# A soft threshold written as a minimum plus a relu of ACT, and weight conversion moved out of the second batch's first stage

## The chip, the cores and the metric

The kernel runs on one core of a Trainium2 chip. The time is that of one execution on the device, in microseconds (us); less is better. A core has five engines with a queue each, worked off in order: PE (matmuls), DVE (vector work), ACT (activations, copies and the issue of some transfers), POOL, and SP, which here only issues transfers. An instruction that waits holds up all that stands behind it in its own queue. Matmuls write to PSUM banks; DVE and ACT carry the results on to SBUF.

## The reference, cut to what matters

```python
X = np.fft.rfft(x, axis=1)                       # x: (2, 3008, 256)
Yr = Xr @ w_r - Xi @ w_i + b_r
Yi = Xr @ w_i + Xi @ w_r + b_i
Y = sign(Y) * max(abs(Y) - 0.01, 0)              # of both parts: the soft threshold
x = np.fft.irfft(Y, n=3008, axis=1)
...
x = (h * clip(h + 3, 0, 6) / 6) @ w_out          # h = x @ w_in, 2048 wide
x = (silu(x @ w_gate) * (x @ w_val)) @ w_out2    # 1536 wide
```

The change lies in the first five lines and in the preparation of the weights `w_in` and `w_out`.

## The kernel before

The Fourier transform of each batch is done in factors. The *first stage* (`pre`, 8 pieces n = 0 to 7 for batch 0 and 8 to 15 for batch 1) multiplies a 96x1024 piece of x with a small table; the two halves of the result are copied from PSUM, half 0 by ACT (L245) and half 1 by DVE (L247), and sent to the scratch tensor Bd. The rest goes in 12 *rounds* p = 0 to 11, six for each batch (`ORDER`), of four frequencies each. The functions of a round:

- `s2` (S): matmuls with a table (L284) in two parts, dh = 0 and 1. For each part ACT makes the high half xh (L288) and its negative (L289), DVE the low half xl (L118), and ACT the negative of that (L291), which is put off to just before the next step by the list `later`.
- `ln` (L), in two halves h: first one step of the weight conversion if any is left, then 24 matmuls (L113 to L115), then on DVE the bias is added (yb, L319), clipped to plus and minus 0.01 (yc, L321) and subtracted (yp, L323).
- `ia` (A), in two halves: matmuls of yp with a table (L330), a copy by ACT (cs, L331), and after the second half the transfer to the scratch tensor Cd (L333).

The order is written out by hand in `seq`. Round p is: L(p) half 0, A(p-1) half 0, a first-stage piece, S(p+1) part 0, S(p+1) part 1, L(p) half 1, a first-stage piece, A(p-1) half 1. First-stage pieces 11 to 15 stand in rounds 0 to 2. From round 8 (`FROM`) on, *units* of the next layer are put between these steps: matmuls ph and acc (L113 to L115), relu r (L430, ACT), product r (L431, DVE), and the split into gh (L449, ACT) and gl (L118, DVE). Just before round 8 stands `post` of the first block (L416), which needs ct, read back from Cd (L404). Batch 1's rounds begin at round 6, so "round 8" is batch 1's third.

*Weight conversion* (`conv1`, 32 pieces) makes two fp32 halves of 64-bit floats. One step works on five pieces at once: DVE makes a piece's low half (L179), ACT another's high half (L175), ACT the mask of the next (L156), DVE the words of one (L164, L165, L166, L172), and SP loads one more (L151). A step runs inside each half of `ln`, inside `pre` for pieces n > 8, and in a unit whenever its weights are due (`conv1.at < 2 * n + 6`), until all is done.

Of the kernel before, what the change touches and what calls it, by code (L numbers as in the profile page):

```python
# [9 lines left out]
F32 = mybir.dt.float32  # L10
# [3 lines left out]
AF = mybir.ActivationFunctionType  # L14
ALU = mybir.AluOpType
# [11 lines left out]
LAM = 0.01  # L27
# [50 lines left out]
def fourier_moe_kernel(ctx: ExitStack, tc: tile.TileContext, x, lin, bias, w1, w2, fwd1, inv2, fwd2,  # L78
                       inv1, out):
    nc = tc.nc  # L80

    def pool(stack, name, side):
        return stack.enter_context(tc.tile_pool(name=name, bufs=1, side=side))
# [28 lines left out]
    def mm3(o, wh, wl, xh, xl, start, stop):  # L112
        nc.tensor.matmul(o, wl, xh, start=start, stop=False)  # L113
        nc.tensor.matmul(o, wh, xl, start=False, stop=False)  # L114
        nc.tensor.matmul(o, wh, xh, start=False, stop=stop)  # L115
# [72 lines left out]
    def pieces(p, name, src, nf, n, into):  # L188
        out = []
        for f in range(nf):  # L190
            t = [p.tile([128, n, 256], F32R, name=f"{name}{i}_{f}") for i in "hl"]
            into[f] = t
            out += [(src[:, f, j], t[0][:, j], t[1][:, j]) for j in range(n)]
        return Convert(out)
# [3 lines left out]
    ap_ = pool(attn_stack, "attn", "right")  # L198
    linh = ap_.tile([128, 2, 2, DIM], F32R, name="linh")
    linl = ap_.tile([128, 2, 2, DIM], F32R, name="linl")  # L200
    bias_sb = ap_.tile([128, DIM], F32, name="bias_sb")

    def ring4(name):
        return ap_.tile([128, 4 * DIM], F32, tag="bc", name=name, bufs=4)


    NT = NJ // 4
    xt = {}

    def load_x(n):  # L210
        b, i = divmod(n, NT)
        if b < NB:
            xt[n] = xs_p.tile([128, 4 * DIM], F32, tag="xah" if n % 2 else "xal", name=f"x{b}_{i}", bufs=2)
            nc.sync.dma_start(xt[n][:QP], x[b][:, i * 4 * DIM : (i + 1) * 4 * DIM])
# [5 lines left out]
    p = psf[0]([128, 512], "p0")  # L220
    for n in range(3):
        nc.tensor.matmul(p, zeros[:, :128], zeros, start=True, stop=True)
    conv1 = pieces(w1p, "w1", w1, KF1, 2, W1)

    def prepare():
        lin_st = ap_.tile([128, 2, 2, DIM], F32, tag="z", name="lin_st", bufs=3)
        nc.gpsimd.dma_start(lin_st, lin)
        nc.gpsimd.dma_start(bias_sb, bias)
        nc.gpsimd.dma_start(inv2_sb, inv2)
        for dh in range(2):  # L230
            for k in range(2):
                hi, lo, st = linh[:, dh, k], linl[:, dh, k], lin_st[:, dh, k]
                nc.gpsimd.tensor_copy(hi, st)
                nc.gpsimd.tensor_tensor(out=lo, in0=st, in1=hi.bitcast(F32), op=ALU.subtract)

    def pre(n):
        b, i = divmod(n, NT)
        load_x(n + 3)
        bs = ring4(f"bs{b}_{i}")
        for h in range(2):  # L240
            p = psf[0]([GW, 512], f"p1_{b}_{i}_{h}")
            nc.tensor.matmul(p, fwd1_sb, xt[n][:QP, h * 512 : (h + 1) * 512], start=True, stop=True)
            o = bs[:GW, h * 512 : (h + 1) * 512]
            if h == 0:
                nc.scalar.copy(o, p)  # L245
            else:
                nc.vector.tensor_copy(o, p)  # L247
        sent()
        out_b.append(lambda: nc.scalar.dma_start(Bd[b][:, i * 4 * DIM : (i + 1) * 4 * DIM], bs[:GW]))
        if i == NT - 1:  # L250
            sent()
# [3 lines left out]
    def sent():  # L255

        for g in out_b:
            g()
        out_b.clear()
# [3 lines left out]
    m_t, z_t, n_t, X, yp, cs = {}, {}, {}, {}, {}, {}  # L263

    def table(tag, src, Q, name, bufs):
        t = ap_.tile([128, 4, 128], F32, tag=tag, name=name, bufs=bufs)
        nc.sync.dma_start(t, src[:, Q * 512 : (Q + 1) * 512].rearrange("r (g c) -> r g c", g=4))
        return t

    def load_q(b, Q):  # L270
        if (b, Q) in z_t or Q >= NQ:
            return
        if Q not in m_t:
            m_t[Q] = table("m", fwd2, Q, f"m{Q}", 6)
        z_t[b, Q] = ap_.tile([128, 4, DIM], F32, tag="z", name=f"z{b}_{Q}", bufs=3)
        nc.sync.dma_start(z_t[b, Q], bview[b][:, Q * 4 : Q * 4 + 4, :])

    def s2(b, Q, dh):

        if dh == 0:  # L280
            X[b, Q] = [ap_.tile([128, 2, 4, 3 * K2], F32R, tag=f"x{k}", name=f"x{k}_{b}_{Q}", bufs=2) for k in "hl"]
        p = psf[0]([128, 4, 128], f"p2_{b}_{Q}_{dh}")
        for g in range(4):
            nc.tensor.matmul(p[:, g, :], z_t[b, Q][:, g, dh * 128 : (dh + 1) * 128], m_t[Q][:, g, :],  # L284
                             start=True, stop=True)
        hi, lo = (t[:, dh, :, K2:] for t in X[b, Q])
        nhi, nlo = (t[:, dh, :, :K2] for t in X[b, Q])
        nc.scalar.copy(hi, p)  # L288
        nc.scalar.mul(nhi, p[:, :, K2:], -1.0)  # L289
        low(lo, p, hi)  # L290
        later.append(lambda: nc.scalar.mul(nlo, X[b, Q][1][:, dh, :, 2 * K2 :].bitcast(F32), -1.0))  # L291

    later = []
# [8 lines left out]
    def ln(b, Q, h):  # L302

        if Q not in n_t:
            n_t[Q] = table("n", inv1, Q, f"n{Q}", 6)
        if not conv1.done():
            conv1.step()
        p = psf[0]([128, 2, DIM], f"p3_{b}_{Q}_{h}")
        xh, xl = X[b, Q]
        for i in range(2):  # L310
            g = 2 * h + i
            n = 0
            for dh in range(2):
                for k, at in ((0, K2), (1, 0)):
                    sl = (slice(None), dh, g, slice(at, at + 128))
                    mm3(p[:, i, :], xh[sl], xl[sl], linh[:, dh, k], linl[:, dh, k], n == 0, n == 3)
                    n += 1
        yb = xs_p.tile([128, 2, DIM], F32, tag="r", name=f"yb{b}_{Q}_{h}", bufs=3)
        nc.vector.tensor_tensor(out=yb, in0=p, in1=bias_sb.unsqueeze(1).to_broadcast([128, 2, DIM]), op=ALU.add)  # L319
        yc = xs_p.tile([128, 2, DIM], F32, tag="r", name=f"yc{b}_{Q}_{h}", bufs=3)  # L320
        nc.vector.tensor_scalar(yc, yb, -LAM, LAM, op0=ALU.max, op1=ALU.min)  # L321
        yp[b, Q, h] = ap_.tile([128, 2, DIM], F32, tag="yp", name=f"yp{b}_{Q}_{h}", bufs=3)
        nc.vector.tensor_tensor(out=yp[b, Q, h], in0=yb, in1=yc, op=ALU.subtract)  # L323

    def ia(b, Q, h):
        if h == 0:
# [14 lines left out]
    def ahead(p):  # L341
        if p < len(ORDER):
            load_q(*ORDER[p])

    def S(p):
        def first():
            ahead(p + 1)
            s2(*ORDER[p], 0)
        return [first, lambda: s2(*ORDER[p], 1)] if p < len(ORDER) else []

    def L(p):
        return [lambda h=h: ln(*ORDER[p], h) for h in range(2)]

    def A(p):
        return [lambda h=h: ia(*ORDER[p], h) for h in range(2)] if p >= 0 else [lambda: None] * 2

    def pre_conv(n):
        pre(n)
        if n > NT:
            conv1.step()  # L360

    P = [lambda n=n: pre_conv(n) for n in range(NB * NT)]
    seq = P[:1] + [prepare] + P[1:NT] + [lambda: load_q(0, 0)] + P[NT : NT + 3] + S(0)
    rest = P[NT + 3 :]
    for p in range(len(ORDER)):
        l, a = L(p), A(p - 1)
        some, rest = rest[:2], rest[2:]
        u = [lambda: unit()] if p >= FROM else []
        seq += [l[0], a[0]] + u + some[:1] + S(p + 1)[:1] + u + S(p + 1)[1:] + [l[1]] + u + some[1:] + [a[1]] + u
        if p == NQ:  # L370
            seq += [lambda: load_ct(blocks[0])]
        if p == FROM - 1:
            seq += [lambda: few.__setitem__(0, True)]
            seq += [lambda: post(blocks[0], 0), lambda: post(blocks[0], 1)]
# [101 lines left out]
    def unit():  # L476

        n = at[0]
        at[0] += 1

        for _ in range(2):
            if conv1.at < 2 * n + 6 and not conv1.done():
                conv1.step()
        if 0 <= n - 1 < len(units):
            lower(units[n - 1])
        if n < len(units):
            k, f = units[n]
            state[units[n]] = project1(k, f, ntok(k))
        if n >= 2:
            outp(units[n - 2])  # L490
        if n < len(units):
            for step in extra.get(units[n], ()):
                step()
        for f in more:
            f(n)
# [303 lines left out]
```

## Time and profile before

| | before |
|---|---|
| time, median of 3 runs (lowest to highest) | 1256.91 us (1256.39 to 1258.61) |
| time of the profiled execution | 1257.64 us |
| its span, first to last instruction | 1255.8 us |
| PE busy | 1233.0 us, 98% |
| DVE busy | 845.7 us, 67% |
| ACT busy | 679.5 us, 54% |
| POOL busy | 6.3 us |
| chain that ended last, by engine | PE 90%, DVE 5%, DMA 2%, ACT 2% |

The shares are averages over stages. The change touches the first 210 us or so, where DVE and ACT feed PE in short steps; the rest of the span is two layers of long matmuls. PE's busy time is modelled from pipelined matmuls, so a PE that reads 98% can still have lost time.

### The profile page before, as it was taken

How to read it: one execution, taken by the hardware profiler on the slowest of the kernel's cores; microseconds unless marked ns; L12 is line 12 of the kernel's file. 1: busy time of each engine (PE TensorE's matmuls, PEld its weight loads, DVE VectorE, ACT ScalarE, POOL GpSimd, SP SyncE). 2: the span in 40 equal slices, each digit the busy share in tenths (PEclk: the TensorE clock that was granted, in tenths of full speed). 3: DMA queues.
4: the chain of work that ended last, by engine and by line, in shares of the span. 5: the costliest groups of instructions: out<-in, count | busy, mean ns of one | idle time of the engine just before them, and what ended most of it. 6: DMA issues, size and time to landing. Idle time of an engine off the chain costs nothing.

```text
span 1255.8 us, 15966 instructions
## 1 busy us (share of the span) xinstructions
PE 1233.0 (98%) x5914; PEld 1035.6 (82%) x5914; DVE 845.7 (67%) x1492; ACT 679.5 (54%) x1216; POOL 6.3 (0%) x15
## 2 busy tenths in 40 slices
PE   8889999999999999999999999999999999999998
PEld 2789898788888888888889878888888888888997
DVE  2588767676666676676666567677676676666665
ACT  2344445455555555555555465566556665555554
POOL 1000000000000000000000000000000000000000
PEclk9899999999999999999999999999999999999999
DMA  9965511231321221232132054554544644544551
GB/s 300 277 220 160 169 42 64 93 99 63 97 95 55 90 89 49 93 99 83 54 104 91 25 212 151 201 187 169 203 166 156 229 171 153 214 153 164 207 184 72
DMA packets 50286, 172.85 MB, mean 138 GB/s; under 512 B 4752, under 2 KB 18160, under 8 KB 39456
## 3 DMA queue, kind: packets, MB, share of 16 engines
q1 hardware_dynamic: 41856, 158.55, 36.7%
q10 hardware_dynamic: 8128, 12.58, 2.9%
q8 instruction: 46, 0.75, 0.2%
q0 software_dynamic: 224, 0.69, 0.2%
q14 instruction: 32, 0.26, 0.1%
HBM read 132.75 MB, written 39.06 MB: 137 GB/s over the span
## 4 chain that ended last, share of the span: by engine, by line
PE 90%; DVE 5%; DMA 2%; ACT 2%; issue 1%; ACTq 0%; DVEq 0%; SPq 0%
PE acc L114 12%; PE acc L115 12%; PE acc L113 12%; PE ph L113 7%; PE ph L115 7%; PE ph L114 7%; PE P L652 5%; PE P L654 5%; PE P L653 5%; PE p L416 3%; PE Tb L652 3%; PE Tb L653 3%; PE Tb L654 3%; PE Q L652 1%; PE Q L654 1%; PE Q L653 1%
## 5 line engine op out<-in xcount | busy, mean ns | idle before, releaser
L118 DVE TENSOR_TENSOR gl<-r,gh 128x512 fp32r<-128x512 f32 (+1 forms) x192 | 130.1, 677 | 79.8 <-ACT gh L449 78.6
L430 ACT ACTIVATE r<-ph,three 128x512 f32<-128x512 f32 (+1 forms) x192 | 130.2, 678 | 96.5 <-PE ph L115 78.3
L431 DVE SCALAR_TENSOR_TENSOR r<-r,ph 128x512 f32<-128x512 f32 (+1 forms) x192 | 129.4, 674 | 61.1 <-ACT r L430 60.4
L449 ACT CAST gh<-r 128x512 fp32r<-128x512 f32 (+1 forms) x192 | 117.4, 611 | 87.5 <-DVE r L431 86.6
L113 PE MATMUL ph<-xah,w1l 128*128 128x512 f32 (+1 forms) x384 | 152.2, 396 | 0.7 <-DVE w1l L179 0.7
L113 PE MATMUL acc<-gh,w1l 128*128 128x512 f32 (+1 forms) x384 | 148.3, 386 | 1.0 <-ACT gh L449 1.0
L114 PE MATMUL acc<-gl,w1h 128*128 128x512 f32 (+1 forms) x384 | 148.3, 386 | 0.6 <-DVE gl L118 0.5
L115 PE MATMUL ph<-xah,w1h 128*128 128x512 f32 (+1 forms) x384 | 148.2, 386 | 0.0
L114 PE MATMUL ph<-xal,w1h 128*128 128x512 f32 (+1 forms) x384 | 148.2, 386 | 0.0
L115 PE MATMUL acc<-gh,w1h 128*128 128x512 f32 (+1 forms) x384 | 148.1, 386 | 0.0
L118 DVE TENSOR_TENSOR gl<-s,gh 128x512 fp32r<-128x512 f32 (+1 forms) x144 | 97.2, 675 | 49.5 <-ACT gh L676 49.5
L652 PE MATMUL P<-xo,slot 128*128 128x512 f32 (+1 forms) x288 | 111.3, 386 | 1.7 <-DVE g L722 0.8
L114 PE MATMUL acc<-gl,slot 128*128 128x512 f32 (+1 forms) x288 | 111.1, 386 | 0.3 <-DVE gl L118 0.2
L113 PE MATMUL acc<-gh,slot 128*128 128x512 f32 (+1 forms) x288 | 111.0, 385 | 0.0
L654 PE MATMUL P<-xo,slot 128*128 128x512 f32 (+1 forms) x288 | 110.9, 385 | 0.0
L653 PE MATMUL P<-xo,slot 128*128 128x512 f32 (+1 forms) x288 | 110.9, 385 | 0.0
L115 PE MATMUL acc<-gh,slot 128*128 128x512 f32 (+1 forms) x288 | 110.9, 385 | 0.0
L718 ACT ACTIVATE s<-g 128x512 f32<-128x512 f32 (+1 forms) x72 | 44.9, 623 | 93.2 <-DVE g L716 93.2
L676 ACT CAST gh<-s 128x512 fp32r<-128x512 f32 (+1 forms) x144 | 88.1, 612 | 1.8 <-DVE s L735 1.6
L114 PEld LDWEIGHTS acc<-gl,w1h 128*128 128x128 f32 x384 | 72.1, 188 | 15.3 <-DVE gl L118 1.7
L113 PEld LDWEIGHTS acc<-gh,w1l 128*128 128x128 f32 x384 | 72.1, 188 | 15.1 <-ACT gh L449 1.5
L113 PEld LDWEIGHTS ph<-xah,w1l 128*128 128x128 f32 x384 | 72.2, 188 | 14.2 <-issue 0.8
(95 smaller groups left out, 2292.9 us busy)
## 6 DMA issues: line engine op xcount, KB each, us to landing
slot<-Wd SPq DMA_DIRECT2D x72, 1152.0 KB, 5.0
st<-in_w SPq DMA_DIRECT2D x68, 256.0 KB, 3.2
Wd<-slot SPq DMA_DIRECT2D x12, 1152.0 KB, 4.7
x<-in_x SPq DMA_DIRECT2D x16, 384.0 KB, 6.2
Bd<-bs ACTq DMA_DIRECT2D x16, 384.0 KB, 5.1
z<-Bd SPq DMA_DIRECT2D x12, 512.0 KB, 5.5
Cd<-cs ACTq DMA_DIRECT2D x12, 512.0 KB, 3.3
Xd<-x SPq DMA_DIRECT2D x20, 256.0 KB, 2.1
```

The source lines that it names most:

```text
L113: nc.tensor.matmul(o, wl, xh, start=start, stop=False)
L114: nc.tensor.matmul(o, wh, xl, start=False, stop=False)
L115: nc.tensor.matmul(o, wh, xh, start=False, stop=stop)
L118: nc.vector.tensor_tensor(out=o, in0=full, in1=hi.bitcast(F32), op=ALU.subtract)
L430: nc.scalar.activation(r[:, :n], p[:, :n], AF.Relu, bias=three)
L431: nc.vector.scalar_tensor_tensor(out=r[:, :n], in0=r[:, :n], scalar=6.0, in1=p[:, :n], op0=ALU.min, op1=ALU.mult)
L449: nc.scalar.copy(hi[:, :n], g[:, :n])
L652: nc.tensor.matmul(o, wl, x[:, 0, :n], start=start, stop=False, skip_group_check=not start)
L653: nc.tensor.matmul(o, wh, x[:, 1, :n], start=False, stop=False, skip_group_check=not start)
L654: nc.tensor.matmul(o, wh, x[:, 0, :n], start=False, stop=True, skip_group_check=not start)
L676: nc.scalar.copy(hi[:, :nb], t[:, :nb])
L718: nc.scalar.activation(s0[:, :n], h, AF.Silu)
```

## The change

Four edits, all in the first two hundred microseconds.

1. The soft threshold is written min(y + 0.01, 0) + relu(y - 0.01). The 0.01 is added to the bias once, on POOL (in `prepare`); DVE adds the bias (yb), ACT makes the relu (yc) with the bias tile `edge2` = -0.02, and DVE joins them with one instruction (yp). That last one is put in the list `later`, which is worked off just before the next step.
2. For batch 1 both halves of a first-stage piece are copied by ACT.
3. `pre` runs no conversion step any more (7 steps, of pieces 9 to 15).
4. Three conversion steps are put behind rounds 3, 5 and 7. The other four of the seven come where units find their weights due.

```diff
+    edge2 = ap_.tile([128, 128], F32, name="edge2")[:, :1]
+    nc.vector.memset(edge2, -2.0 * LAM)
...
+        nc.gpsimd.tensor_scalar(bias_sb, bias_sb, LAM, None, op0=ALU.add)
...
-            if h == 0:
+            if h == 0 or b:
                 nc.scalar.copy(o, p)
             else:
                 nc.vector.tensor_copy(o, p)
...
-        nc.vector.tensor_scalar(yc, yb, -LAM, LAM, op0=ALU.max, op1=ALU.min)
+        nc.scalar.activation(yc, yb, AF.Relu, bias=edge2)
...
-        nc.vector.tensor_tensor(out=yp[b, Q, h], in0=yb, in1=yc, op=ALU.subtract)
+        later.append(lambda: nc.vector.scalar_tensor_tensor(out=yp[b, Q, h], in0=yb, scalar=0.0, in1=yc, op0=ALU.min, op1=ALU.add))
...
     def pre_conv(n):
         pre(n)
-        if n > NT:
-            conv1.step()
...
+        if p in (3, 5, 7):
+            seq += [lambda: conv1.step()]
```

PE's order is the same in both. Where DVE and ACT change, row by row:

DVE between the second half of L in round 3 (yb_3_1) and the first half of round 4 (yb_4_0), before:

```order
L319 TENSOR_TENSOR yb_3_1_850<-p_0_3_1_825,bias_sb 128x512
L321 TENSOR_SCALAR yc_3_1_852<-yb_3_1_850 128x512
L323 TENSOR_TENSOR yp_3_1_854<-yb_3_1_850,yc_3_1_852 128x512
L179 TENSOR_TENSOR w1l_127<-wt,w1h_126 128x256
L164 TENSOR_SCALAR wt<-st 128x256
L165 SCALAR_TENSOR_TENSOR wt<-st,wt 128x256
L166 SCALAR_TENSOR_TENSOR wt<-st,wt 128x256
L172 SCALAR_TENSOR_TENSOR wt<-mask,wt 128x256
L319 TENSOR_TENSOR yb_4_0_899<-p_0_4_0_874,bias_sb 128x512
```

The same place in the changed kernel, from yp_3_1 on (line numbers are those of the changed file, up to four higher):

```order
L327 SCALAR_TENSOR_TENSOR yp_3_1_780<-yb_3_1_776,yc_3_1_778 128x512
L179 TENSOR_TENSOR w1l_123<-wt,w1h_122 128x256
L164 TENSOR_SCALAR wt<-st 128x256
L165 SCALAR_TENSOR_TENSOR wt<-st,wt 128x256
L166 SCALAR_TENSOR_TENSOR wt<-st,wt 128x256
L172 SCALAR_TENSOR_TENSOR wt<-mask,wt 128x256
L179 TENSOR_TENSOR w1l_123<-wt,w1h_122 128x256
L164 TENSOR_SCALAR wt<-st 128x256
L165 SCALAR_TENSOR_TENSOR wt<-st,wt 128x256
L166 SCALAR_TENSOR_TENSOR wt<-st,wt 128x256
L172 SCALAR_TENSOR_TENSOR wt<-mask,wt 128x256
L323 TENSOR_TENSOR yb_4_0_836<-p_0_4_0_811,bias_sb 128x512
```

Two conversion steps stand there instead of one, and DVE's instruction yc is gone; yp still stands right behind yb.

ACT at the start of round 3, before: its last conversion rows, the copy cs of A(2), and xh of S(4).

```order
L175 CAST w1h_126<-wt 128x256
L156 ACTIVATE mask<-st 128x256
L331 COPY cs_2_785<-p_0_2_0_786 128x512
L288 CAST xh_4_794<-p_0_4_0_796 128x4x128
L289 ACTIVATE xh_4_794<-p_0_4_0_796 128x4x64
L291 ACTIVATE xl_4_795<-xl_4_795 128x4x64
L288 CAST xh_4_794<-p_0_4_1_805 128x4x128
```

The same in the changed kernel:

```order
L175 CAST w1h_120<-wt 128x256
L156 ACTIVATE mask<-st 128x256
L325 ACTIVATE yc_3_0_707<-yb_3_0_705,edge_107 128x512
L335 COPY cs_2_711<-p_0_2_0_712 128x512
L291 CAST xh_4_720<-p_0_4_0_722 128x4x128
L292 ACTIVATE xh_4_720<-p_0_4_0_722 128x4x64
L294 ACTIVATE xl_4_721<-xl_4_721 128x4x64
L291 CAST xh_4_720<-p_0_4_1_731 128x4x128
```

The relu stands ahead of the copy cs and of xh, and it reads what DVE's yb wrote.

DVE in round 10 (batch 1, names yb_4_0 and xl_5), where the units run beside it, before:

```order
L319 TENSOR_TENSOR yb_4_0_1778<-p_1_4_0_1753,bias_sb 128x512
L321 TENSOR_SCALAR yc_4_0_1780<-yb_4_0_1778 128x512
L323 TENSOR_TENSOR yp_4_0_1782<-yb_4_0_1778,yc_4_0_1780 128x512
L118 TENSOR_TENSOR gl<-r,gh 128x512
L431 SCALAR_TENSOR_TENSOR r<-r,ph 128x512
L118 TENSOR_TENSOR xl_5_1810<-p_1_5_0_1811,xh_5_1809 128x4x128
L118 TENSOR_TENSOR gl<-r,gh 128x512
```

And in the changed kernel:

```order
L327 SCALAR_TENSOR_TENSOR yp_4_0_1741<-yb_4_0_1737,yc_4_0_1739 128x512
L179 TENSOR_TENSOR w1l_139<-wt,w1h_138 128x256
L164 TENSOR_SCALAR wt<-st 128x256
L165 SCALAR_TENSOR_TENSOR wt<-st,wt 128x256
L166 SCALAR_TENSOR_TENSOR wt<-st,wt 128x256
L172 SCALAR_TENSOR_TENSOR wt<-mask,wt 128x256
L118 TENSOR_TENSOR gl<-r,gh 128x512
L435 SCALAR_TENSOR_TENSOR r<-r,ph 128x512
L118 TENSOR_TENSOR xl_5_1780<-p_1_5_0_1781,xh_5_1779 128x4x128
```

A conversion step now stands between yp and gl. Behind this xl follow two more, and a fourth behind the next soft threshold (yb_4_1); before, these four had been done by the end of round 2.

## Rows read from the trace of the kernel before

**Rows 1.** Stretches: length; busy PE, PEld, DVE, ACT, POOL; PE clock, DMA share, GB/s.

```profile
40.29:74.49 34.20, 34.20 (x222) 28.27 (x222) 27.61 (x61) 14.53 (x36) 0.00 (x0) 1.00 0.82 260
74.49:79.28 4.79, 1.24 (x8) 0.83 (x7) 3.38 (x9) 2.69 (x8) 0.00 (x0) 1.00 0.90 300
119.18:129.18 10.00, 9.42 (x71) 8.86 (x72) 8.35 (x19) 4.90 (x12) 0.00 (x0) 1.00 0.60 176
173.88:198.67 24.79, 24.79 (x147) 21.85 (x145) 19.53 (x41) 13.63 (x29) 0.00 (x0) 1.00 0.21 64
```

**Rows 2.** The chain that ended last: start us, us, what.

```profile
29.00 5.40 DMA z<-Bd
...
83.20 0.86 PE p L330 x4
84.06 1.78 PE p L284 x16
...
92.46 0.87 PE p L330 x4
```

**Rows 3.** Timeline of DVE, one round: start us, us, instruction, shapes [idle before <-releaser].

```profile
111.08 0.68 DVE L319 TENSOR_TENSOR yb<-p,bias_sb 128x512 f32<-128x512 f32 x1
...
112.87 0.42 DVE L179 TENSOR_TENSOR w1l<-wt,w1h 128x256 fp32r<-128x256 f32 x1
...
114.86 0.68 DVE L319 TENSOR_TENSOR yb<-p,bias_sb 128x512 f32<-128x512 f32 x1
...
116.04 0.69 DVE L323 TENSOR_TENSOR yp<-yb,yc 128x512 f32<-128x512 f32 x1
116.64 0.68 DVE L118 TENSOR_TENSOR xl<-p,xh 128x512 fp32r<-128x512 f32 x1
118.57 0.69 DVE L118 TENSOR_TENSOR xl<-p,xh 128x512 fp32r<-128x512 f32 x1 [1.24 <-ACT xh L289]
...
121.09 0.68 DVE L319 TENSOR_TENSOR yb<-p,bias_sb 128x512 f32<-128x512 f32 x1
```

**Rows 4.** Timeline at rounds 2, 3 and 8: S of PE, two yb of DVE.

```profile
68.96 1.95 PE L284 MATMUL p<-m,z 128*128 128x128 f32 x16
...
84.83 0.68 DVE L319 TENSOR_TENSOR yb<-p,bias_sb 128x512 f32<-128x512 f32 x1
...
136.00 0.68 DVE L319 TENSOR_TENSOR yb<-p,bias_sb 128x512 f32<-128x512 f32 x1
```

**Rows 5.** Groups of ACT and DVE, 36 to 212 us: busy us, mean ns, idle before.

```profile
L331 ACT COPY cs<-p 128x512 f32<-128x512 f32 x22 | 12.7, 578 | 16.5 <-PE p L330 16.5
L430 ACT ACTIVATE r<-ph,three 128x512 f32<-128x512 f32 x16 | 10.9, 684 | 10.5 <-DVE yp L323 9.1 <-PE ph L115 1.4
L449 ACT CAST gh<-r 128x512 fp32r<-128x512 f32 x15 | 9.2, 614 | 2.6 <-DVE r L431 2.1 <-ACT cs L331 0.4
...
L321 DVE TENSOR_SCALAR yc<-yb 128x512 f32<-128x512 f32 x24 | 10.2, 427 | 0.8
```

**Rows 6.** Timeline of ACT in one round: xh, and the negative of xl.

```profile
113.61 0.59 ACT L288 CAST xh<-p 128x512 fp32r<-128x512 f32 x1 [0.30 <-PE p L284]
114.09 0.39 ACT L289 ACTIVATE xh<-p 128x256 fp32r<-128x256 f32 x1
...
117.36 0.42 ACT L291 ACTIVATE xl<-xl 128x256 fp32r<-128x256 f32 x1 [2.88 <-DVE xl L118]
```

**Rows 7.** Timeline: Cd sent by ACT, and PE's first use of what is read back.

```profile
120.84 0.37 ACTq L333 DMA_DIRECT2D Cd<-cs  x1
...
128.66 0.77 PE L416 MATMUL p<-inv_sb,ct 96*128 96x94 f32 x5 [0.44 <-ACT xh L289]
```

**Rows 8.** Groups of DVE, 173.88 to 198.67 us: columns as in rows 5.

```profile
L118 DVE TENSOR_TENSOR gl<-r,gh 128x512 fp32r<-128x512 f32 x4 | 2.7, 686 | 1.0 <-ACT gh L449 1.0
...
L118 DVE TENSOR_TENSOR xl<-p,xh 128x512 fp32r<-128x512 f32 x2 | 1.4, 691 | 2.3 <-ACT xh L289 2.3
```

**Rows 9.** Timeline of PE where round 10's units wait.

```profile
199.24 0.47 PE L113 MATMUL ph<-xah,w1l 128*128 128x512 f32 x1 [0.41 <-DVE w1l L179]
```

## The prediction

> **What bounds it now.** I read the stretches first, then the chain that ended last, then DVE's and ACT's own timelines. Until 74.5 us PE is never idle: 34.20 us busy of 34.20 [rows 1]. Then it stands: from 74.49 to 79.28 it works 1.24 us. That is the start of round 3, where DVE has fallen behind. From there on the rounds follow DVE, not PE. The reader should see it in two places. PE's own pace, right after the stall, is 92.46 - 83.20 = 9.26 us a round [rows 2]. But DVE starts the same yb 10.01 us apart, at 111.08 and 121.09 [rows 3], and PE is busy for only 9.42 of 10.00 us there [rows 1].
>
> DVE is not full either: 8.35 of 10.00 us [rows 1]. It is a loop of DVE and ACT without PE in it: soft threshold 1.79 (111.08 to 112.87), conversion 1.99, soft threshold 1.78 (114.86 to 116.64), then xl, whose second part starts 1.93 later because DVE idles 1.24 us for ACT's xh (116.64 to 118.57), then 2.52 for that xl and the next conversion [rows 3]. The second xl's slot being 0.6 like yp's (116.04 to 116.64), that conversion takes 1.91, so a step is about 1.95.
>
> From round 8 on PE is the bound again, with DVE idle for 24.79 - 19.53 = 5.26 us between 173.88 and 198.67 [rows 1]. At 199.24 PE waits 0.41 us for a weight half that DVE made [rows 9]: DVE has just run out of its lead.
>
> **Part 1: DVE freed in rounds 0 to 2.** Five copies of half a piece leave DVE there, some 0.7 us each like yp [rows 3] (three more leave it earlier, before round 0), and seven conversion steps, some of them partial. PE was full in that stretch, so nothing is won before 74.5. What is won is the stall. Where does DVE reach yb of round 3? S(3) starts on PE at 68.96 [rows 4]; its first part ends some 0.9 later, ACT's xh and its negative take 0.48 + 0.39 [rows 6], so xl starts near 70.8 and the second at 72.7. Add its slot 0.6, a conversion without its low half (1.95 less 0.3), a soft threshold (2.07, below), a step 1.95: 79.0, against 84.83 before [rows 4]. **DVE gains 5.8 us**, and no more, as PE ends that half of round 3 only at 77.4 (74.49 and 24 matmuls; a round of 9.26 less 1.78 for S and twice 0.86 for A leaves 2.9 for each half of L [rows 2]). ACT is busy 14.53 of 34.20 us there [rows 1], which hides its five extra copies.
>
> **Part 2: the relu on ACT.** DVE loses yc, 0.43 us [rows 5]. But yp stands right behind yb in DVE's queue, so DVE now idles while ACT works. The relu of 512 elements from SBUF with a bias tile is not in the trace. From below: a copy from PSUM, 0.58. From above: the copy from SBUF, 0.61, plus what relu with a bias tile costs over a copy from PSUM (0.684 - 0.578 = 0.11), 0.72 [rows 5]. The second has the same source and bias, so I take it. From yb's start to yp's then is 0.68 + 0.72 and two hand-overs of 0.03 (xl ends at 116.64 + 0.68, ACT begins at 117.36 [rows 3, 6]), 1.46; with yp's slot of 0.6, 2.07 to the next instruction: 0.28 more than 1.79.
>
> The first half costs more. In ACT's queue the relu stands ahead of the copy cs and of xh for S. Before, xh was ready when DVE came to xl. Now ACT starts the relu 0.72 after yb began, and xl has to wait for relu, cs, xh and the negative: 0.61 + 0.48 + 0.48 + 0.39 start to start (the 0.72 and 0.58 less the 0.11 by which xh and its negative overlap [rows 6]), 0.03 more: 2.71 from yb to xl instead of 1.78, so 0.93 more. **A round's loop grows by 0.28 + 0.93 = 1.2 us, to 11.2.** With the lower bound it is 0.95; if ACT has still another instruction like the negative (0.39) in front of each relu, 2.0. Five rounds, 3 to 7: 6.0 us (4.7 to 10). The copies cs, behind the relu too, come later (part 5).
>
> The Trainium skill (Perfetto Trace Analysis, Optimizing Scalar/DVE Operations) says that offloading some work to Scalar may make sense where DVE is saturated. By it the round would lose two yc, 0.92 us, and the whole would end at 1254 (rival A). The row speaks against it: DVE is at 8.35 of 10.00, and its wait is for ACT. The skill's ScalarE: Activation LUTs (Rules for kernel authors) would keep relu, min and max on VectorE; that is the loop's side of it.
>
> **Part 3: three steps behind rounds 3, 5 and 7.** They enter that same loop: 3 x 1.95 = 5.85 us. Their cover would be DVE idle time, but the 1.24 us is a hand-over between two xl and no step fits there.
>
> **Part 4: at no cost.** The addition on POOL and one memset lie tens of us ahead of their use; without cover, under 1 us. The loads of the moved steps leave SP's queue behind z of round 0, whose transfer of 5.40 us [rows 2] round 0 waits for; they stand after it in the queue, so I take 0 (bounds: 1 us of the 5.40 gained if they slow it now, 0.3 lost if the tiles behind it come in another order). yp as one instruction lasts what the subtraction lasted. Putting it in the list moves it past nothing.
>
> **Part 5: how the lag reaches PE.** On DVE the yb of round 8, 136.00 before [rows 4], comes at -5.8 + 6.0 + 5.85 = 6.05 later. PE feels it first at L416, which needs Cd of batch 0 read back. ACT sends it behind cs, at 120.84, and PE starts at 128.66 [rows 7]. In the change that cs stands behind the relu of round 6's second half. Its yb comes at 121.09 - 5.8 + 3.6 + 3.9 + 0.93 = 123.7, the relu 0.72 later, cs 0.61 after that and the transfer 0.6 after cs: 125.7, **4.8 us late**. The units that follow take gl and xal from a DVE that is 6.05 late. What they have to spare no single row tells; I take the middle of the two, 5.4 for PE (4.0 to 6.5). From then on PE is the bound and DVE catches up.
>
> **Part 6: round 10.** Four conversion steps, 7.8 us, and three soft thresholds at 0.28 enter between 173.9 and 199. DVE's idle time takes up between 3.3 us (xl and gl alone, 2.3 + 1.0 [rows 8]) and all 5.26 [rows 1]. So DVE comes 3.4 to 5.3 later to the place where PE already waits 0.41 for it [rows 9]. I take 4.0, near the lower end, as some steps fall in idle time that opens when ACT falls back.
>
> **Sum.** 5.4 + 4.0 = 9.4 us slower. The profiled execution took 1257.64, so 1267.0; it lies 0.73 above the median of the runs (1256.91), so **1266**. What a measurement of this kernel can tell from no change is about 0.2%, 2.5 us.
>
> **Rivals.** *A, faster: ACT's relu costs DVE no wait.* The loop falls by 0.92 a round; yb of round 8 comes at -5.8 - 4.6 + 5.85 = -4.55. Round 10 then costs 7.8 - 3 x 0.46 less 4.6 of idle time (between the two ends above), +1.8. Together -2.7: 1254. It decides from a loop shorter than 9.7 us. For it: ACT is under half busy in the loop, 4.90 of 10.00 [rows 1]. Against: nothing stands between yb and yp to fill the wait. *B: the first lag is mostly swallowed,* because PE has reserves in front of the units that I can't see; then about half of the 5.4 and the 4.0: 1263. *C: the change hardly matters:* relu at the lower bound, round 10's steps in idle time: 4.7 for the relu, so yb +4.7, of which PE feels little, and little in round 10: 1257 to 1259. *D: a busier ACT.* The relu waits behind what ACT has in hand, and if each relu meets a busy ACT (2.0 a round, not 1.2) 4 us come on top: 1270.
>
> **How the numbers follow.** My forecast (1262.5 to 1269.5) 0.55, B 0.13, D 0.10, C 0.09, A 0.13. Faster by over 0.2% is A, 0.13; within it C, 0.09; slower the rest, 0.78. The range from 1255 leaves out A, and to 1271.5 the far half of D: less than 2 in 10.
>
> **What would show it.** In the profile after: no stall of PE near 74.5; DVE idle for ACT's yc some 0.75 us in each soft threshold and for xh before *both* xl; yb of rounds 3, 4, 5 at about 79, 92 and 103; Cd of batch 0 sent near 125.7 and L416 near 133.5; PE waiting for w1l or gl by 4 us around round 10. I would be wrong if yb to xl stays under 2 us, if the rounds 4 to 7 come nearer to 9.3 than to 11 us, or if PE goes on without waits while DVE is 6 us late.

## The result, and the profile after

| | before | after |
|---|---|---|
| time, median (lowest to highest) | 1256.79 us (1256.39 to 1258.61, 4 runs) | 1268.2 us (1267.06 to 1269.4, 4 runs) |
| ratio to before, with 95% interval | | 1.0088 (1.0071 to 1.0106) |
| time and span of the profiled execution | 1257.64 and 1255.8 us | 1269.4 and 1267.6 us |

The changed kernel is 11.4 us slower by the medians; forecast were 9.1. First the stretches of the changed kernel: length; busy PE, PEld, DVE, ACT, POOL; PE clock, DMA share, GB/s.

```profile
40.05:74.25 34.20, 34.20 (x224) 28.49 (x225) 14.34 (x26) 18.80 (x41) 0.00 (x0) 1.00 0.75 245
74.25:79.30 5.05, 5.05 (x42) 4.94 (x41) 4.08 (x10) 2.59 (x7) 0.00 (x0) 1.00 0.61 175
117.00:128.24 11.24, 8.92 (x57) 8.06 (x56) 7.61 (x18) 6.15 (x14) 0.00 (x0) 0.85 0.30 107
181.60:205.10 23.50, 22.16 (x135) 19.27 (x134) 20.90 (x50) 14.65 (x34) 0.00 (x0) 1.00 0.36 101
```

Against [rows 1]: in rounds 0 to 2 DVE's work has halved, from 27.61 to 14.34 us of 34.20, and the stall behind them is gone, PE works 5.05 of 5.05 us. But a round that took 10.00 us now takes 11.24, though DVE works *less* in it, 7.61 us instead of 8.35. In round 10 it is DVE that is nearly full now, 20.90 of 23.50. PE's clock of 0.85 in the third row is not what makes that round long: round 4 (92.53 to 103.77) ran at 0.70 and took the same 11.24 us.

Where the longer round goes stands in DVE's timeline of round 6, the one that answers to [rows 3]:

```profile
116.99 0.68 DVE L323 TENSOR_TENSOR yb<-p,bias_sb 128x512 f32<-128x512 f32 x1
118.46 0.69 DVE L327 SCALAR_TENSOR_TENSOR yp<-yb,yc 128x512 f32<-128x512 f32 x1 [0.79 <-ACT yc L325]
119.71 0.69 DVE L118 TENSOR_TENSOR xl<-p,xh 128x512 fp32r<-128x512 f32 x1 [0.55 <-ACT xh L292]
121.64 0.69 DVE L118 TENSOR_TENSOR xl<-p,xh 128x512 fp32r<-128x512 f32 x1 [1.24 <-ACT xh L292]
...
124.16 0.68 DVE L323 TENSOR_TENSOR yb<-p,bias_sb 128x512 f32<-128x512 f32 x1
125.69 0.69 DVE L327 SCALAR_TENSOR_TENSOR yp<-yb,yc 128x512 f32<-128x512 f32 x1 [0.85 <-ACT yc L325]
...
128.22 0.69 DVE L323 TENSOR_TENSOR yb<-p,bias_sb 128x512 f32<-128x512 f32 x1
```

The bracket at a row's end is DVE's idle time and who ended it. One wait has become four: 0.79 and 0.85 us for the relu, 0.55 more for the first xh. ACT's side of the first two, where [rows 6] showed xh without anything ahead of it:

```profile
117.71 0.72 ACT L325 ACTIVATE yc<-yb,edge 128x512 f32<-128x512 f32 x1 [2.15 <-DVE yb L323]
118.34 0.56 ACT L335 COPY cs<-p 128x512 f32<-128x512 f32 x1
118.81 0.59 ACT L291 CAST xh<-p 128x512 fp32r<-128x512 f32 x1
119.28 0.40 ACT L292 ACTIVATE xh<-p 128x256 fp32r<-128x256 f32 x1
```

ACT idles 2.15 us, then makes relu, cs and xh in one go, while DVE idles. The two engines take turns.

The chain that ended last (start us, us, what) went from DVE over ACT to PE's matmuls `post` before, with no transfer in it:

```profile
126.65 0.69 DVE xl L118
...
128.26 0.29 ACT xh L289
128.66 2.84 PE p L416 x24
```

Now it runs through ACT's copy cs and the two transfers behind it, and it ends in PE's late start, the place of [rows 7]:

```profile
124.24 0.61 DVE yb L323
125.00 0.56 issue
125.57 0.57 ACT cs L335
126.16 2.84 DMA Cd<-cs
129.02 4.51 DMA ct<-Cd
133.66 4.67 PE p L420 x24
```

Cd leaves 5.3 us later than before (126.16, 120.84) and PE begins post 5.0 later (133.66, 128.66). From round 10 on, between 182 and 239.5 us, the waits of PE are, in total us, times and longest:

```profile
PE ph L113 <- DVE w1l L179: 3.9, 3, 2.2
PE acc L114 <- DVE gl L118: 0.5, 2, 0.3
```

The same stretch before, 174 to 227.3 us:

```profile
PE ph L113 <- DVE w1l L179: 0.7, 2, 0.4
PE acc L114 <- DVE gl L118: 0.3, 1, 0.3
```

PE waits 3.4 us more for DVE there. The place of [rows 9], where PE waited 0.41, is now at 211.00 and shows 2.17; a unit ahead of it, where PE did not wait before, shows 1.09.

### The profile page after: what moved, and what is told of

Its sections match the earlier page's. It is cut to its first block, busy times and chain, and to the rows that moved or that the text cites. A ratio compares the mean times of both kernels' runs of the same rounds, so it can differ in the third digit from the quotient of the medians.

```text
span 1267.6 us, 15961 instructions
## 1 busy us (share of the span) xinstructions
PE 1238.0 (98%) x5914; PEld 1040.0 (82%) x5914; DVE 831.6 (66%) x1461; ACT 698.4 (55%) x1248; POOL 7.1 (1%) x16
## 4 chain that ended last, share of the span: by engine, by line
PE 87%; DVE 6%; DMA 4%; ACT 2%; issue 1%; SPq 0%; ACTq 0%; DVEq 0%
PE acc L114 11%; PE acc L115 11%; PE acc L113 11%; PE ph L113 7%; PE ph L115 6%; PE ph L114 6%; PE P L656 5%; PE P L658 5%; PE P L657 5%; PE p L420 3%; PE Tb L656 3%; PE Tb L658 3%; PE Tb L657 3%; PE Q L656 1%; PE Q L658 1%; PE Q L657 1%
```

## Experiments

Theory 1 is the prediction's: the relu on ACT makes DVE idle and puts xh and cs behind it, so that a round's loop of DVE and ACT grows by 1.2 us; the moved steps then cost again in that loop and in round 10. Each expectation names its rivals. Ratios are to the kernel before on the same chip, with 95% intervals.

**The relu back on DVE** (the changed kernel otherwise, so edits 2 to 4 alone).

```diff
-        nc.scalar.activation(yc, yb, AF.Relu, bias=edge2)
+        nc.vector.tensor_scalar(yc, yb, -2.0 * LAM, 0.0, op0=ALU.add, op1=ALU.max)
```

> Edit 1's relu goes back to DVE (the sum with -0.02 and the maximum with 0 in one instruction), edits 2 to 4 stay. Theory 1 (DVE waiting for ACT's relu, and xh behind it, cost 1.2 us a round, and the moved conversion steps cost 1.95 each): rounds 3 to 7 go back to 10 us a round plus three steps; yb of round 8 then comes within 0.5 us of before, PE reaches L416 within 1 us of before and does not fall to the lower clock there; round 10's four steps still cost 3 to 4 us. 1260 us (1258.5 to 1262). Theory 2 (the moved steps are the whole cost, the relu is harmless): 1266 to 1269. Theory 3 (the relu is the whole cost): 1256 to 1258.

1260.34 us, ratio 1.0020 (1.0011 to 1.0029): theory 1's number. The starts of DVE's yb in this kernel:

```profile
90.49 0.68 DVE L323 TENSOR_TENSOR yb<-p,bias_sb 128x512 f32<-128x512 f32 x1
...
100.50 0.69 DVE L323 TENSOR_TENSOR yb<-p,bias_sb 128x512 f32<-128x512 f32 x1
...
112.51 0.68 DVE L323 TENSOR_TENSOR yb<-p,bias_sb 128x512 f32<-128x512 f32 x1
```

A round is 10.01 us again, and 12.01 with a moved step behind it. So the relu's place is worth 1268.2 - 1260.3 = 8 us of the changed kernel's loss, and the moved steps cost in the loop what one step lasts. One item was off: PE begins post at 126.10, 2.6 us earlier than in [rows 7], where within 1 us was expected. The four steps of round 10 by themselves cost 3.7 us here: PE's A of that round is 1.6 us early (171.87, before 173.45), its next post 2.1 late (240.08, before 237.93).

**The relu alone** (the kernel before with edit 1; against the changed kernel the diff is as below).

```diff
-            if h == 0 or b:
+            if h == 0:
...
+        if n > NT:
+            conv1.step()
...
-        if p in (3, 5, 7):
-            seq += [lambda: conv1.step()]
```

> The kernel before with edit 1 alone (relu on ACT, both copies split between ACT and DVE, conversion steps in the first stage as before). Theory 1: 1.2 us a round in rounds 3 to 7 and some 2 us in rounds 0 to 2, so yb of round 8 about 8 us late, L416 6 to 8 us late, up to 3 us more for PE's lower clock after that wait, and 1 us in round 10: 1266 us (1263 to 1269). Theory 2 (relu harmless): 1256 to 1258.

1270.17 us, ratio 1.0106 (1.0089 to 1.0122): the relu alone costs more than all four edits. The direction is theory 1's; the size is 4 us over the expected value and 1 us above its range. The rounds are 11.25 us as expected, and yb of round 8 comes 9.0 us late (145.0, against 136.00 in [rows 4]). PE begins post 7.4 us late (136.04) and then runs at 0.60 and 0.64 of its clock in two stretches of 4.5 us, so that its first A in round 8 is 10.5 late (144.8, before 134.3); from round 10 to its next post another 1.1 are added. These are the terms that the expectation lists (6 to 8, up to 3, 1): they came out near their upper ends, and the 1266 was too low a sum of them. DVE's groups for three of its rounds, 92.5 to 126.3 us, show the price (busy us, mean ns, idle before):

```profile
L327 DVE SCALAR_TENSOR_TENSOR yp<-yb,yc 128x512 f32<-128x512 f32 x6 | 4.2, 692 | 4.9 <-ACT yc L325 4.9
L118 DVE TENSOR_TENSOR xl<-p,xh 128x512 fp32r<-128x512 f32 x6 | 4.1, 691 | 5.4 <-ACT xh L292 5.4
```

Idle in each round: 4.9 / 3 = 1.63 us for the relu, 5.4 / 3 = 1.80 for xh (1.24 before); saved in each round: two yc, 0.85. That is 1.63 + 0.56 - 0.85 = 1.3 us net, and 1.25 were measured.

**ACT's copies alone** (the kernel before with edit 2).

```diff
-            if h == 0:
+            if h == 0 or b:
                 nc.scalar.copy(o, p)
```

> The kernel before with edit 2 alone (batch 1's first stage copied by ACT). Theory 1: DVE sets the pace from round 0 to round 7, so the five copies of 0.7 us that leave it in rounds 0 to 2 come off the time almost whole: 1253.5 us (1252.5 to 1254.5), yb of round 8 3.4 us earlier. Rival (the stretch to 74.5 us is PE's, and the loop behind it goes its own way): no change, 1256 to 1257.5.

1256.04 us, ratio 0.9985 (0.9976 to 0.9994): a small gain, 1.5 us on the same chip, less than half of what I expected. The time lies in the rival's range and not in theory 1's, but its path is theory 1's: yb of round 3 starts at 82.67, 2.2 us earlier than in [rows 4], and yb of round 8 at 133.86, 2.1 earlier. The rounds between are 10.0 us as before. Of the 3.4 us of five copies another 0.8 are hidden by this execution's later start (first S at 35.32 us, before at 34.53).

In the profiled execution PE then keeps this lead of 2.0 us up to 214 us and loses it by 238 (next post at 238.03, before 237.93). At 226.28 PE waits 1.61 us for ACT's gh, where it waited 1.05 before, and behind that wait the clock falls (columns of the stretches; before, then this kernel):

```profile
227.70:232.40 4.70, 4.44 (x18) 3.44 (x19) 3.84 (x8) 3.30 (x6) 0.00 (x0) 1.00 0.06 19
226.30:231.00 4.70, 4.47 (x12) 3.32 (x13) 3.86 (x8) 2.67 (x5) 0.00 (x0) 0.64 0.02 7
```

The longer wait takes 0.6 us of the lead, the slower matmuls 1.5. This execution is the slowest of the ten (1257.48; the others 1254.12 to 1256.89); whether the others had the same fall no trace shows.

**A step in the wait** (the changed kernel; the conversion step that stood ahead of the matmuls of each half of L now stands between yb and yp, its rows on ACT move behind the relu with it, and yp no longer goes through the list).

```diff
-        if not conv1.done():
-            conv1.step()
         p = psf[0]([128, 2, DIM], f"p3_{b}_{Q}_{h}")
...
         nc.scalar.activation(yc, yb, AF.Relu, bias=edge2)
...
+        if not conv1.done():
+            conv1.step()
+        nc.vector.scalar_tensor_tensor(out=yp[b, Q, h], in0=yb, scalar=0.0, in1=yc, op0=ALU.min, op1=ALU.add)
```

> The changed kernel with the conversion step of each half of L put between yb and yp, so that DVE has 1.95 us of work while ACT makes the relu; the same instructions otherwise. Theory 1 (it is the wait, and xh's place behind it, not the work): the loop falls to about 9.1 us, below PE's 9.28, or 11.05 where a step was added behind a round; yb of round 8 some 4.6 us earlier than before the change; round 10 costs about 2: 1254 us (1251 to 1257). Rival (ACT is too busy, or the moved steps are the cost): 1264 to 1269.

1257.82 us, ratio 1.0004 (0.9994 to 1.0014): 10 us better than the changed kernel and level with before, but short of the 1254 and just outside its range. The mechanism shows: a round is 9.0 us where no moved step stands (yb at 89.9 and 98.9), and 11.0 with one. The moved steps still cost, and the next kernels take them out.

**The steps back in the first stage** (the changed kernel without edits 3 and 4; relu and copies of ACT stay).

```diff
+        if n > NT:
+            conv1.step()
...
-        if p in (3, 5, 7):
-            seq += [lambda: conv1.step()]
```

> The changed kernel with edits 3 and 4 undone: the seven conversion steps run in the first stage again, the relu of ACT and ACT's copies stay. Theory 1 (the relu holds DVE and ACT's queue up, 11.25 us a round, and that sets the end): the relu alone came out at 1270.2, the copies alone gained 2.1 us at yb of round 3, so 1267 (1265 to 1269), rounds 4 to 7 at 11.25 us each, PE standing at the first matmul after ct. Theory 2 (the steps in rounds 3 to 7 and in round 10 are what costs): about 1258 to 1261.

1266.53 us, ratio 1.0072 (1.0059 to 1.0086): theory 1's number. With a DVE that waits for the relu anyhow, moving the steps costs only 1.7 us, and the intervals of the two ratios overlap. What the three steps lose in rounds 3 to 7 had been won in rounds 0 to 2: without the move yb of round 3 comes 3.4 us later than in the changed kernel (82.72, 79.30), and yb of round 8 still 0.8 later (143.44, 142.63). In round 10 the four steps show apart. From PE's A of that round to the end of round 11's work, the lag grows by 0.9 us here (PE 182.40 against 173.45 before, ACT's mask of the next layer's conversion 236.60 against 226.74), and by 4.1 in the changed kernel (181.59 and 238.95). The steps are 3.2 of these 4.1.

**The steps back, and one in the wait** (the two edits above together).

> The kernel before it, and besides the conversion step of each half of a round stands between yb and yp, so that DVE works while ACT makes the relu. Theory 1: DVE's loop falls to 9.0 us as it did with the moved steps, PE's 9.28 is the bound of rounds 4 to 7; yb of round 8 and Cd come as in that experiment (about 132 and 118.5), but round 10 has no steps to take in, which cost 2.9 there: 1254.5 (1252 to 1257). Theory 3 (something else in the changed arrangement of DVE and ACT after round 8 costs the 2.9, not the four steps): 1257 to 1259.

1250.10 us (1249.79 to 1252.48, 5 runs), ratio 0.9946 (0.9933 to 0.9958). This is faster than both kernels, by 7.2 us against before and by 18 against the changed one; it is 4 better than expected and below the expected range. DVE at the start of round 3:

```profile
77.67 0.68 DVE L321 TENSOR_TENSOR yb<-p,bias_sb 128x512 f32<-128x512 f32 x1
78.27 0.41 DVE L179 TENSOR_TENSOR w1l<-wt,w1h 128x256 fp32r<-128x256 f32 x1
...
80.25 0.69 DVE L327 SCALAR_TENSOR_TENSOR yp<-yb,yc 128x512 f32<-128x512 f32 x1
81.02 0.69 DVE L118 TENSOR_TENSOR xl<-p,xh 128x512 fp32r<-128x512 f32 x1
```

No bracket stands at yp or at the first xl: the step of 1.98 us covers relu, cs and xh. Its stretches (columns as above):

```profile
74.30:79.30 5.00, 5.00 (x41) 4.87 (x40) 4.86 (x12) 3.15 (x7) 0.00 (x0) 1.00 0.84 283
104.00:113.25 9.25, 9.25 (x75) 9.03 (x74) 7.46 (x17) 6.01 (x16) 0.00 (x0) 1.00 0.58 173
```

PE is busy without a gap at 74.5 as in the rounds, which take 9.25 us, PE's own 9.26 [rows 2]. The 1254.5 took yb of round 8 and Cd from the kernel with the step in the wait (about 132 and 118.5), whose rounds 3, 5 and 7 still had a moved step each; without these they come at 127.46 and 113.80. Post begins at 121.64, 7.0 us earlier than in [rows 7]. Beside the kernel with the step in the wait and edits 3 and 4, at 1.0004, this gives those two edits' price where DVE does not idle: 0.0058 of 1257 us, 7.3 us.

**PE kept working until ct comes** (the changed kernel, two matmuls of zeros ahead of post).

```diff
+            def hold():
+                p = psf[0]([128, 512], "hold")
+                for n in range(2):
+                    nc.tensor.matmul(p, zeros[:, :128], zeros, start=True, stop=True)
+            seq += [hold]
             seq += [lambda: post(blocks[0], 0), lambda: post(blocks[0], 1)]
```

> The changed kernel, with two matmuls of zeros put in PE's queue right ahead of the first matmul that reads ct, which fill most of PE's 1.69 us wait there. Theory 1c (the stand lets the clock fall, and the slower 9 us behind it make PE 3 us later than the late ct alone): the 24 matmuls take 2.9 us instead of 4.67, the clock of the next 9 us is above 0.95, and as DVE is then the later one (6.6 us late at round 8, where PE was 8.1), 1266.3 (1265.0 to 1267.0). Rival: the slow stretch is hidden behind DVE, or the clock falls all the same: 1268 (1267.4 to 1269).

1268.04 us, ratio 1.0085 (1.0071 to 1.0099): the rival's number, the total doesn't move. What the edit was to do, it did (each of the two matmuls shows as two rows, x4):

```profile
131.89 1.88 PE L381 MATMUL hold<-zeros 128*128 128x512 f32 x4
134.43 2.84 PE L425 MATMUL p<-inv_sb,ct 96*128 96x94 f32 x24 [0.66 <-DVE xl L118]
```

The 24 matmuls take 2.84 us where the changed kernel's chain shows 4.67, and PE is through with round 8's first half of L 2.4 us earlier (its A at 140.06 instead of 142.43). But then PE waits for DVE and ACT, from 134.5 to 182 us (total us, times, longest; the 0.66 ahead of post is left out):

```profile
PE acc L113 <- ACT gh L458: 0.7, 1, 0.7
...
PE acc L114 <- DVE gl L118: 0.3, 1, 0.3
```

In the changed kernel that view is empty from 134 to 182: there PE was the later one, and in round 8 ACT waited for it (first row the relu r, second xh):

```profile
144.89 0.69 ACT L434 ACTIVATE r<-ph,three 128x512 f32<-128x512 f32 x1 [0.33 <-PE ph L115]
145.78 0.59 ACT L291 CAST xh<-p 128x512 fp32r<-128x512 f32 x1 [0.20 <-PE p L287]
```

Here both rows stand without a bracket (145.14 and 145.72), and round 8 is shorter on DVE, 8.85 us from yb to yb (143.33 to 152.18) instead of 9.61 (142.63 to 152.24). So 0.8 us of the clock's price reach DVE. This execution had reached round 3 0.8 us later than the changed one (80.09, 79.30), ahead of the edit, and yet PE's A of round 10 comes 0.8 earlier (180.80, 181.59). So up to 1.6 us of the clock's price may be real; the medians, 0.2 us apart, can't tell that from nothing.

**A relu that nobody reads** (the changed kernel, yp without yc).

```diff
-        later.append(lambda: nc.vector.scalar_tensor_tensor(out=yp[b, Q, h], in0=yb, scalar=0.0, in1=yc, op0=ALU.min, op1=ALU.add))
+        later.append(lambda: nc.vector.scalar_tensor_tensor(out=yp[b, Q, h], in0=yb, scalar=0.0, in1=yb, op0=ALU.min, op1=ALU.add))
```

> The changed kernel, but yp is made from yb twice and doesn't read the relu, so the threshold's upper part is left out of the output; ACT makes the relu all the same, in the same place of its queue. It splits the 1.25 us by which a round grew. Theory 1: DVE's own wait goes (0.8 us in each half), but xh and xl still stand behind the relu in the first half, so only the second half's 0.85 and perhaps some of the first are won: rounds of 10.2 to 10.5 us without a moved step. Total about 1261 (1259 to 1263.5). Rival (the wait between yb and yp is everything): rounds of 9.3 us, PE's own pace, and 1256 or less. Rival (ACT's queue is everything): rounds still 11.25, 1268.

1264.11 us, ratio 1.0049 (1.0036 to 1.0061). A round is 10.5 us (yb at 91.5 and 102.0), at the edge of theory 1's 10.2 to 10.5, and both one-sided rivals (9.3, 11.25) are out; the total is 0.6 above the expected range. The first half of a round:

```profile
102.00 0.68 DVE L323 TENSOR_TENSOR yb<-p,bias_sb 128x512 f32<-128x512 f32 x1
102.72 0.69 DVE L327 SCALAR_TENSOR_TENSOR yp<-yb 128x512 f32<-128x512 f32 x1
104.72 0.69 DVE L118 TENSOR_TENSOR xl<-p,xh 128x512 fp32r<-128x512 f32 x1 [1.31 <-ACT xh L292]
```

yb to xl is 2.72 us, as in the changed kernel (116.99 to 119.71), though DVE waits nowhere for the relu. In the first half ACT's queue alone sets the pace; the wait of DVE counts in the second half, 0.75 us.

**The filled relu without the copies** (the kernel of 1250.1 us with `if h == 0:` again).

> The kernel that came out at 1250.1 (relu of ACT, conversion steps back in the first stage, one step of each half between yb and yp), but with the copies of batch 1's first stage as before, half by ACT and half by DVE. Theory 1 (the filled wait is what wins: 0.43 us of DVE for each half of a round, from round 0 on): rounds of 9.2 to 9.3 us, and of the stall near 77 a third comes back, since DVE gets five copies of 0.7 us again: 1251.5 (1250 to 1253.5). Rival (the gain needs the copies on ACT; the relu is worth little by itself): 1255 to 1257.

1253.29 us (1250.96 to 1255.05), ratio 0.9965 (0.9951 to 0.9979): within the range, at its upper part. It does the same work on each engine as "the relu alone", 1270.17 us (PE 5914, DVE 1469 and ACT 1240 instructions in both); only one conversion step of each half stands behind yb instead of ahead of the matmuls. That place is worth 17 us. Of the stall near 77 nearly half is left, not a third: PE waits 1.7 us for xl up to 100 us, before 3.6.

## Why the prediction was right

The forecast held in its direction and its mechanism; one term was too small and the errors add up to 2.3 us.

- **Part 1** (yb of round 3 at 79.0): 79.30, and no stall is left near 74.5. Rounds 4 and 5 follow at 92.53 and 103.77 (forecast 92 and 103).
- **Part 2** (the relu 0.72 us, 2.71 from yb to xl, loop 11.2): 0.72, 2.72, 11.25. The Trainium skill, ScalarE: Activation LUTs, section "What ACT_TABLE_LOAD costs", gives 280 ns + 0.833 ns an element for an activation with a bias tile, by estimate 0.707 us for 512: the trace agrees, with 0.72. The experiments with the unread relu and with DVE's relu show the two waits apart.
- **Part 3** (1.95 a moved step): rounds of 13.2 us with one, 11.25 without (yb at 103.77, 116.99, 128.22).
- **Part 4** (nothing): no stretch shows a cost. The first S starts at 34.28 us, before at 34.53, and between 32.8 and 35.3 in the other kernels' profiled executions.
- **Part 5, the mis-sized term** ("5.4 for PE (4.0 to 6.5)"): Cd left at 126.16 and post began at 133.66, where the text had 125.7 and 133.5, and DVE reached round 8 at 142.63, 6.6 late, where it had 6.05. But PE's A of round 8 comes 8.1 us late (142.43, before 134.29) and stays that late until round 10. I took PE's lag to lie between ct's 4.8 and DVE's 6.05. Two things came on top, one for each engine. PE stood 1.69 us and then ran mostly at its lower clock: post begins 5.0 us late, and by the A the slower matmuls have made 8.1 of it; the text had no term for that. And DVE's round 8 is longer too, 9.61 us from yb to yb where it was 8.09 (136.00 to 144.09), so that its second half is also 8.1 late. About half of that growth is the relu, which stays when the matmuls of zeros hold the clock (8.85); the other half hangs on the slow PE, for which ACT waits there. So the count "five rounds, 3 to 7" was short by about 0.8 us, and the clock's price came on top. With the zeros PE's A of round 8 is 5.8 late (140.06), and by round 9 waits for DVE and ACT have made 7.4 of it (159.20, before 151.84).
- **Part 6** (4.0): 4.1 from PE's A of round 10 on. 0.9 of it come with the relu alone and 3.2 with the four steps on top; the steps alone, with the relu on DVE, cost 3.7.
- **Sum**: 8.1 + 4.1 = 12.2, and the span grew by 11.8. Part 5 left its own bounds by 1.6 us; the total stayed in the forecast range because that is 7 us wide and the other terms were close.

Rival A needed a loop under 9.7 us and got 11.25; what the text had against it, that nothing stands between yb and yp, is what decided: with a step there the loop is 9.0. A's time does not come with it, as all four edits then took 1257.82 us and not 1254; a gain came only with the steps back in the first stage (1250.10 and 1253.29). The Trainium skill (Perfetto Trace Analysis, Optimizing Scalar/DVE Operations) says that offloading some work to Scalar may make sense if DVE is saturated. The runs bear that out only where the wait is filled: the relu on ACT, with nothing else changed but that place, gave 0.9965 with a step in the wait and 1.0106 without. B and C fall, as no lag was swallowed. D's time is near (1270), its mechanism is not: the relu starts 0.72 us after yb began, with no instruction ahead of it.

What stays open: how much of the changed kernel's time the clock alone costs (0.2 us by the medians, up to 1.6 by one execution), and 0.4 of the 3.4 us that the copies alone were to give at round 3.

## What to carry to other kernels

An instruction that is moved to a less busy engine takes its consumer's wait along: the result costs two hand-overs and whatever stands in the other queue, so independent work of at least that length has to stand between producer and consumer on the first engine. Here that place, with the same work on every engine, made the difference between 1.1% slower and 0.4% faster. And work that is moved out of a full stretch should go where its engine idles *after* the other edits: rounds 0 to 2, which lost the seven steps, had DVE at 14.34 of 34.20 us in the end, while the places that took them had no room: in rounds 3 to 7 the loop of DVE and ACT set the pace, and in round 10 DVE was at 20.90 of 23.50.

## What the runs showed of the hardware

PE's clock fell after a short stand. In the changed kernel PE waits 1.69 us for ct, and the next 9 us read (columns of the stretches):

```profile
133.60:138.10 4.50, 4.44 (x24) 4.47 (x25) 3.55 (x9) 2.54 (x6) 0.00 (x0) 0.59 0.58 202
138.10:142.60 4.50, 4.50 (x27) 4.50 (x27) 4.29 (x11) 2.04 (x6) 0.00 (x0) 0.65 0.84 275
```

0.59 and 0.65 are means of the two levels, 1.2 and 2.4 GHz. PE's row is full in both, and yet it does less: the 24 matmuls of post take 4.67 us instead of 2.84, a matmul of L 0.41 instead of 0.28. With 1.88 us of matmuls on zeros in the gap, and 0.66 us idle behind them, the clock stayed at 1.00 in the same stretches.

It is not the only such fall. The kernel before shows one behind its stall at 74.5, where PE waited 2.69 and 0.86 us:

```profile
79.28:84.00 4.72, 4.72 (x23) 4.61 (x24) 4.48 (x12) 2.25 (x6) 0.00 (x0) 0.64 0.56 160
```

What a fall cost here went by which engine was the later one. In rounds 4 and 6 of the changed kernel it cost nothing, as DVE and ACT set the pace (11.24 us at 0.70 as at 0.85). Behind post the slower matmuls made 3.1 us of PE's lag, but with the clock held DVE and ACT kept at least 1.5 of them. In the profiled execution of "ACT's copies alone" nothing hid it behind 226 us, and PE lost 1.5 us.
